# Finch attention with a mixture of adapters on one core: tile 22's scaled r and k transposed by DMA, and the order planned anew

## The chip, the cores and the metric

The kernel runs on one core of a Trainium2 chip. A core has a matrix engine (TensorE: PE for its matmuls, PEld for its weight loads), VectorE (DVE), ScalarE (ACT), GpSimd (POOL), and SyncE (SP), which here only issues DMAs. The metric is the device time of one execution in microseconds; 85.32 us is the median of three before the change.

## The reference

```python
def _attn_ref(r, k, v, w, u):                  # (4, 8, 768, 48) each, u (8, 48)
    state = np.zeros((B, H, D, D))
    for t in range(S):
        cur = einsum('bhd,bhe->bhde', u[None] * kt, vt)
        y[:, :, t] = einsum('bhd,bhde->bhe', rt, state + cur)
        state = wt[:, :, :, None] * state + einsum('bhd,bhe->bhde', kt, vt)

def _moe_ref(x, w_gate, A, B):                 # x = y as (3072, 384); E = 8, rank 16
    logits = x @ w_gate
    # the two largest of 8, softmax over the two
    delta[token] += w_e * ((x @ A[e]) @ B[e])  # for both chosen e
    return x + delta
```

## The kernel before

The 4 x 768 tokens are 24 tiles of 128; six tiles make one sequence (NCHUNK), so the state is started anew at tiles 0, 6, 12 and 18. All work of one tile is cut into small steps. A step is a function, and `PLAN`, a string in the file, lists every step as `name:tile` or `name:tile.variant`; the variant is mostly the engine. The program is emitted in exactly that order, so each engine works through its own steps in the order of the list, and waits where a step's inputs or its buffer are not ready. There is no other scheduling: the list is the schedule.

Steps of one tile t, with their lines:

- `load_w` (L182, L192, from SP), `load_rk` (L203) and `load_v` (L211, both issued by POOL, with a cast to fp16) bring in groups of 2 to 8 tiles; `ln` (ACT, L233, L238) takes the logarithm of w.
- `csA` and `csB` (PE, L245 to L254) sum log w along the tile in a PSUM bank, `expP` and `expN` (ACT, L259, L263) take the exponentials of it and of its negative.
- `mult` (VectorE, L284; L269 in two halves for tiles 0 and 1, there also as `multr`, `multk`) scales r and k by them into one of four buffers `rk2`.
- The scaled r and k must be transposed. `tr` (PE, L332) does it with eight transposes into the PSUM tile `trp`, and `trev` copies that to `rkT` on ACT (L309) or VectorE (variant 1, L311). For some tiles `trd` (L338) does both at once: one DMA transpose on SP's queue, from `rk2` to `rkT`.
- `amm` (PE, L353) multiplies k and r to `a_ps`, which has one buffer; `aev` (VectorE, L359) masks it to `at`; `kv` (PE, L366) adds to the state, `sev` copies the state out (ACT L303, VectorE L305), `szero` (POOL, L382) clears the blocks of the other head.
- `rkp` (L293) is the product r k, on POOL or VectorE (variant 1). `xk` (PE, L421) transposes it together with the result of three tiles earlier, `xkev` copies both out (ACT L309, VectorE L311), `dg` (PE, L298) and `dgev` (L303, L305) give the u term, and `dv` (POOL, L322) multiplies it with v.
- `ymS` (L387) and `ymA` (L397) make y on PE; `ba` (L403) adds dv there with a matmul in variant 1. `xs` is the finished attention row: on ACT (L411) after such a `ba`, else on VectorE, which adds dv to y (L413).
- Mixture: `lg` (PE, L436) makes the logits. For each of eight batches of 4, 4, 4, 4, 4, 2, 1 and 1 tiles follow `g1` (VectorE, from L446), `gexp` (ACT, L461), `g2` to `g4`, `z` (PE, L497), `zw` (VectorE, L505, L510), `zTm` (PE, L520), `zTev` (L309, L311). Then each tile has `d` (PE, L533, L534), `oev` (ACT L303, VectorE L542 or L305) into one of six `res` buffers, and `store` (SP, L546).
- `warm` (PE, L173) are matmuls on constants that keep PE running at the start.

`y_ps`, `xk_ps`, `z_ps`, `zT_ps` and `d_ps` share three PSUM buffers in turn, so such a step waits until the third tile before it in the list has been read out.

```python
    def trd(t, ch):
        x = wk.tile([128, 2, P, 128], BF16, name="rkT", bufs=4)
        nc.sync.dma_start(out=x.rearrange("p m q f -> p (m q) f"),
                          in_=st[t]["rk2"].rearrange("s m p h d -> s (m p h d)"), transpose=True)
```

Of the kernel before, what the change touches and what calls it, by code (L numbers as in the profile page):

```python
# [33 lines left out]
csB:3 expN:3 aev:1 tr:2 ymA:0 kv:2 xk:-1 dv:0.1 ba:0.1 load_rk:12 ln:4 ymS:1 szero:1 ymA:1 trev:2.1 xkev:-1 csA:4
dg:2 xs:0.1 amm:2 rkp:3.1 expP:4 mult:3 xk:0 aev:2 load_w:6 load_v:12 csB:4 sev:2 xkev:0 rkp:4.1 expN:4 tr:3 dg:3
kv:3 csA:5 dv:1.1 trev:3 dgev:3.1 ymS:2 amm:3 expP:5 ymA:2 dv:2.1 ba:1.1 csB:5 mult:4 ln:6 rkp:5 tr:4 sev:3.1 expN:5
aev:3 load_rk:16 xs:1.1 csA:6 trev:4 xk:1 szero:2 expP:6 load_w:8 ba:2.1 amm:4 xs:2.1 mult:5 dv:3 lg:0 szero:3.1
csB:6 tr:5 aev:4 load_w:10 xk:2 expN:6 csA:7 trev:5.1 ymS:3 load_v:16 xkev:1 xkev:2 ymS:4 dg:5 expP:7 ln:8 ymA:3
mult:6 ba:3 dg:4 csB:7 expN:7 load_w:12 rkp:6 amm:5 tr:6 xs:3 xk:3 dgev:5.1 kv:4 lg:2 dv:4 load_w:14 csA:8 trev:6
aev:5 ymA:4 ba:4 sev:4.1 amm:6 expP:8 lg:1 rkp:7 xs:4 szero:4 xkev:3 dv:5.1 csB:8 kv:6 mult:7 lg:3 g1:3 xk:4 expN:8  # L40
ymS:5 csA:9 dg:6 rkp:8 ln:12 xkev:4.1 tr:7 aev:6 load_w:16 expP:9 gexp:3 dg:7 load_B:0 ymA:5 trev:7 z:3 g2:3 ba:5.1
csB:9 dgev:7.1 sev:6 mult:8 expN:9 load_w:18 xs:5.1 amm:7 kv:7 g3:3 lg:4 csA:10 tr:8 ymA:6 sev:7 expP:10 trev:8 kv:8
xk:5 dv:6 aev:7 rkp:9 ba:6 csB:10 g4:3.1 mult:9 tr:9 sev:8 szero:7 kv:9 zw:3 zTm:3 dv:7.1 expN:10 xs:6 zTev:3 csA:11
szero:6 xkev:5 xk:6 trev:9 expP:11 amm:8 ymS:7 xkev:6 mult:10 szero:8 ba:7.1 csB:11 ymA:7 expN:11 dg:9 dg:8 rkp:10
tr:10 aev:8 sev:9.1 xs:7.1 castB:0 csA:12 expP:12 amm:9 ymS:8 dgev:9.1 mult:11 trev:10 xk:7 dv:8 aev:9 rkp:11 csB:12
ymA:8 expN:12 load_w:20 lg:6 tr:11 szero:9 ba:8 d:3.2 xkev:7 trev:11 xs:8 csA:13 lg:7 expP:13 lg:5 oev:3.2 g1:7 d:1
xk:8 csB:13 oev:1 xkev:8.1 expN:13 dv:9 amm:10 d:2 mult:12 ymS:9 csA:14 ba:9 kv:10 dg:10 gexp:7 ymS:10 g2:7 ln:16
ymA:9 aev:10 rkp:13.1 dg:11 dgev:11 tr:12 expP:14 sev:10 oev:2 rkp:12 xs:9 amm:11 dv:10.1 ymA:10 csB:14 aev:11
trev:12.1 expN:14 lg:8 kv:12 mult:13 ba:10.1 rkp:14.1 xs:10.1 g3:7 xk:9 csA:15 d:0.2 szero:10 xk:10 xkev:9 dg:12
expP:15 xkev:10 mult:14 dv:11.1 amm:12 oev:0.2 g4:7 sev:12 szero:12 csB:15 tr:13 expN:15 ymS:11 kv:13 dg:13 ba:11.1  # L50
trev:13 ymA:11 sev:13 csA:16 z:7 xs:11.1 expP:16 tr:14 dgev:13 mult:15 aev:12 zw:7 xk:11 load_w:22 store:0 csB:16
amm:13 lg:10 zTm:7 ymA:12 dv:12 xkev:11.1 ln:20 ba:12 kv:14 lg:11 expN:16 lg:9 trev:14 csA:17 aev:13 dv:13.1 rkp:15
g1:11 ymS:13 zTev:7.1 xs:12 ba:13.1 mult:16 expP:17 sev:14 tr:15 ymA:13 amm:14 xs:13.1 csB:17 gexp:11 xk:12 rkp:16
d:5 szero:13 g2:11 expN:17 xkev:12 xk:13 rkp:18 trev:15 csA:18 trd:16 dg:15 aev:14 expP:18 g3:11 g4:11 dg:14 mult:17
oev:5 z:11 amm:15 csB:18 store:3 dgev:15 kv:15 xkev:13 szero:14 ymS:14 dv:14 rkp:17.1 d:6 expN:18 ymA:14 dv:15 zw:11
csA:19 ba:14 aev:15 sev:15 oev:6 lg:12 ymS:15 szero:15 dg:16 kv:16 lg:13 ymA:15 expP:19 csB:19 ba:15 xs:14 expN:19
amm:16 rkp:19 xk:14 mult:18 zTm:11 sev:16 xs:15 csA:20 kv:18 d:4 xkev:14 aev:16 rkp:21 trd:17 zTev:11.1 xk:15 dg:17
store:1 amm:17 expP:20 ymS:16 oev:4 mult:19 dgev:17 sev:18 ymA:16 csB:20 kv:19 d:8.2 store:2 rkp:22.1 dv:16.1
xkev:15 trd:18 dv:17.1 lg:14 d:11 aev:17 expN:20 ba:16.1 sev:19 csA:21 oev:8.2 mult:20 trd:19 amm:18 xs:16.1 expP:21
lg:15 xk:16 d:9.2 dg:18 csB:21 oev:11 aev:18 szero:16 oev:9.2 ymS:17 rkp:20 ba:17.1 store:5 ymA:17 xkev:16 trd:20  # L60
expN:21 dg:19 kv:20 xs:17.1 amm:19 store:6 csA:22 xk:17 sev:20 szero:19 szero:18 dgev:19 dv:18 mult:21 expP:22 lg:16
kv:21 d:10 xkev:17 ymA:18 csB:22 ba:18 ymS:19 dv:19 aev:19 oev:10 ymA:19 d:7 ba:19 amm:20 g1:15 xs:18 expN:22 xs:19
xk:18 trd:21 gexp:15 xk:19 sev:21 csA:23 oev:7 dg:20 xkev:18 xkev:19 store:9 expP:23 szero:20 rkp:23 ymS:20 lg:17
# [534 lines left out]
```

## Time and profile before

| | before |
|---|---|
| median of 3 runs (lowest, highest) | 85.32 us (85.1, 86.31) |
| the profiled execution | 85.61 us |
| its span, first to last instruction | 83.9 us |
| instructions | 3133 |
| moved by DMA | 19.10 MB |
| granted TensorE clock, mean | 0.988 |

The profile gives for each group of instructions its count, busy time, mean duration and the idle time of the engine just ahead of it. Its times are microseconds from the first instruction. An operation on VectorE begins before the one ahead of it has ended in the record, so durations add up to more than the span; where the order is judged, the distance from one start to the next is the measure. The busy time of PE is modelled from its pipeline and says little on how full it is.

### The profile page before, as it was taken

The page shows a single profiled execution, that of the slowest core. Times are in us where ns is not written, and L with a number is a line of the kernel's source. Part 1 is how long each engine was busy: PE and PEld are TensorE (multiplying, and loading weights), DVE is VectorE, ACT ScalarE, POOL GpSimd, SP SyncE. Part 2 cuts the span into 40 slices and gives each one's busy share as a digit, 9 for nine tenths or more (in the row PEclk, how much of TensorE's full clock was granted, in tenths as well). Part 3 has the DMA queues.
Part 4 walks back from the last instruction along what each step waited for, and adds up shares of the span by engine and source line. Part 5 has one row for each costly group of instructions (what it writes and reads, how often), then busy time and mean ns, then how long its engine had stood idle before and what let it go on. Part 6 is the DMA issues. An engine that isn't in the chain of part 4 may idle for free.

```text
span 83.9 us, 3133 instructions
## 1 busy us (share of the span) xinstructions
PE 76.5 (91%) x1214; PEld 56.8 (68%) x1214; DVE 72.1 (86%) x166; ACT 68.3 (81%) x163; POOL 57.1 (68%) x113
## 2 busy tenths in 40 slices
...
GB/s 13 328 388 283 272 289 281 275 272 293 282 211 214 262 254 252 287 293 283 226 212 212 208 225 55 221 295 140 125 200 225 204 289 90 99 281 109 277 250 129
DMA packets 15407, 19.10 MB, mean 228 GB/s; under 512 B 7200, under 2 KB 12320, under 8 KB 15392
## 3 DMA queue, kind: packets, MB, share of 16 engines
...
q8 instruction: 9, 0.15, 0.7%
...
## 4 chain that ended last, share of the span: by engine, by line
PE 76%; DVE 6%; ACT 6%; DMA 4%; issue 2%; DVEq 1%; ACTq 0%
PE xk_ps L421 10%; PE trp L332 8%; PE a_ps L353 8%; PE y_ps L397 5%; PE cs_ps L254 5%; PE z_ps L497 4%; PE d_ps L534 4%; PE cs_ps L250 4%; PE a_ps L173 4%; DMA w<-in_w_dram 4%; PE s_ps L366 4%; PE y_ps L387 4%; PE cs_ps L245 4%; PE d_ps L533 3%; PE y_ps L403 2%
## 5 line engine op out<-in xcount | busy, mean ns | idle before, releaser
L359 DVE TENSOR_TENSOR at<-a_ps,strict 128x1024 f16<-128x1024 f32 x24 | 29.3, 1220 | 1.2 <-PE a_ps L353 0.8
L322 POOL TENSOR_TENSOR dv<-v,dg 128x384 f16<-128x384 f16 (+1 forms) x24 | 20.4, 859 | 8.6 <-ACT dg L303 4.7
L293 POOL TENSOR_TENSOR rkp<-rk 128x384 f16<-128x384 f16 (+1 forms) x16 | 14.6, 916 | 0.8 <-DMA rk<-in_rk_dram 0.7
L263 ACT ACTIVATE e<-cs_ps 128x384 bf16<-128x384 f32 x24 | 11.9, 494 | 3.3 <-PE cs_ps L254 3.0
L259 ACT ACTIVATE e<-cs_ps 128x384 bf16<-128x384 f32 x24 | 12.1, 503 | 1.6 <-PE cs_ps L250 1.4
L284 DVE TENSOR_TENSOR rk<-rk,e 128x768 bf16<-128x768 f16 x22 | 12.8, 582 | 0.0
L332 PE MATMUL trp<-ident,rk 128*128 128x128 bf16 x144 | 11.1, 219 | 0.4 <-DVE rk L284 0.4
L309 ACT COPY xkT<-xk_ps 128x384 f32<-128x384 f32 (+1 forms) x24 | 10.5, 447 | 0.9 <-PE xk_ps L421 0.6
L382 POOL MEMSET S_sb<- 64x192 bf16 x38 | 9.6, 252 | 2.4 <-DVE S_sb L305 0.5
L332 PEld LDWEIGHTS <-rk 128*128 128x128 bf16 x144 | 9.0, 97 | 2.0 <-DVE rk L284 0.8
L353 PE MATMUL a_ps<-rkT 48*128 48x128 bf16 x192 | 9.5, 219 | 0.1
L309 ACT COPY rkT<-trp 128x512 f32<-128x512 f32 x15 | 9.0, 597 | 0.0
L397 PE MATMUL y_ps<-v,at 128*128 128x48 f16 x192 | 8.7, 183 | 0.0
L250 PE MATMUL cs_ps<-logw,strict 128*128 128x384 f16 x24 | 8.0, 332 | 0.6 <-ACT logw L233 0.6
L303 ACT COPY res<-d_ps 128x384 f32<-128x384 f32 x15 | 7.2, 488 | 1.5 <-PE zT_ps L520 0.9
L353 PEld LDWEIGHTS <-rkT 48*128 48x128 bf16 x192 | 5.5, 94 | 4.1 <-issue 1.8
L293 DVE TENSOR_TENSOR rkp<-rk 128x384 f16<-128x384 f16 (+1 forms) x8 | 3.8, 472 | 5.1 <-DMA rk<-in_rk_dram 5.1
L254 PE MATMUL cs_ps<-logw,ident 128*128 128x384 f16 x24 | 8.0, 335 | 0.2 <-ACT e L259 0.2
L421 PE MATMUL xk_ps<-ident,rkp 128*128 128x128 f16 x72 | 8.0, 220 | 0.0
L421 PE MATMUL xk_ps<-ident,xs 128*128 128x128 f16 x72 | 8.0, 219 | 0.0
L397 PEld LDWEIGHTS <-at 128*128 128x128 f16 x192 | 7.3, 96 | 0.9
L534 PE MATMUL d_ps<-Ball,zT 128*128 128x384 f16 x24 | 7.8, 327 | 0.0
...
## 6 DMA issues: line engine op xcount, KB each, us to landing
...
w_in<-in_w_dram SPq DMA_DIRECT2D x8, 384.0 KB, 13.0
rk<-in_rk_dram POOLq DMA_DIRECT2D x5, 384.0 KB, 14.5
...
w<-in_w_dram SPq DMA_DIRECT2D x3, 384.0 KB, 9.1
v<-in_v_dram POOLq DMA_DIRECT2D x3, 384.0 KB, 18.7
rk<-in_rk_dram POOLq DMA_DIRECT2D x1, 768.0 KB, 21.2
...
```

The lines of the kernel that those rows point to most:

```text
L254: nc.tensor.matmul(cs_ps[:, 0:HD], lhsT=ident16, rhs=st[t]["logw"], start=False, stop=True, skip_group_check=True)
L259: nc.scalar.activation(out=e2[:, 0], in_=cs_ps[:, 0:HD], func=ACT.Exp)
L263: nc.scalar.activation(out=st[t]["e2"][:, 1], in_=cs_ps[:, 0:HD], func=ACT.Exp, scale=-1.0)
L284: nc.vector.tensor_mul(rk2s[t % 4].rearrange("s m p h d -> s (m p h) d")[:, :, 0:D], st[t]["rk"].rearrange("s m (h d) -> s (m h) d", d=D), ...
L293: (nc.gpsimd, nc.vector)[ch].tensor_mul(x, st[t]["r"], st[t]["k"])
L309: nc.scalar.copy(out=out.bitcast(F32), in_=in_.bitcast(F32))
L322: (nc.gpsimd, nc.gpsimd, nc.vector)[ch].tensor_mul(x, st[t]["v16"], st[t]["dg"].rearrange("p (h o) -> p h o", o=1).to_broadcast([L, H, D]))
L332: nc.tensor.transpose(trp[:, m, p, :], st[t]["rk2"][:, m, p, :, :].rearrange("s a b -> s (a b)"), ident)
L353: nc.tensor.matmul(a_ps[:, g, p, :], lhsT=rkT[base:base + D, 1, p, :], rhs=rkT[base:base + D, 0, p, :], start=True, stop=True)
L359: nc.vector.tensor_mul(at, st[t]["a_ps"].rearrange("s g p f -> s (g p) f"), strict.to_broadcast([128, H, 128]))
L397: nc.tensor.matmul(y_ps[:, h, :], lhsT=st[t]["at"][:, g * P + p, :], rhs=st[t]["v16"][:, h, :], start=(c == 0 and h == 0), stop=(h == H - ...
L421: nc.tensor.transpose(xk_ps[:, 3 * q + j, :], src[:, j * 128:(j + 1) * 128], ident16)
```

## The change

Only `PLAN` is edited; no function changes. `tr:22` and `trev:22` go and `trd:22` comes, so that tiles 16 to 22 are transposed by DMA, and 0 to 15 and 23 by PE. All other steps are the same, but their order is new from the first word to the last, and many have another variant. On VectorE are now 14 `rkp` (8 before), 6 `xkev` (3), 3 `sev` (5), 1 `trev` (3), 11 `xs` (12), 8 `oev` (9) and 6 `dgev` (4); POOL has 10 `rkp` (16). The order of POOL's loads among themselves is kept; SP has `load_B` ahead of `load_w:12`. The start and the end of the list:

```diff
-load_w:0 setD:0 warm:0.5 load_w:1.1 load_rk0:1.1 mask_co:0 mask_ident16:0 mask_strict:0 load_v:0 load_rk0:0 table:0
-load_rk:2 ln:0 ln:1 csA:0 warm:1.2 rkp:0.1 load_v:2 expP:0 csB:0 warm:2.3 setid:0 load_rk:4 padD:0 expN:0 multr:0
-load_rk:6 csA:1 warm:3.3 expP:1 csB:1 warm:4.3 multk:0 tr:0 load_w:2 load_wt:0 kv:0 expN:1 ln:2 trev:0 rkp:1
-load_v:4 mult:1 sev:0.1 load_rk:8 csA:2 xk:-3 warm:5.1 load_w:4 amm:0 expP:2 xk:-2 casts:0 load_v:8 csB:2 aev:0 tr:1
...
-aev:20 g2:15 dg:21 lg:18 lg:19 store:7 mult:22 dgev:21 store:11 dv:20.1 amm:21 csB:23 kv:22 z:15 store:10 store:4
-ymA:20 ba:20.1 tr:22 g3:15 ymS:21 expN:23 g4:15 aev:21 xs:20.1 ymA:21 zw:15 dv:21 mult:23 ba:21 xk:20 trev:22 zTm:15
-xkev:20 amm:22 zTev:15.1 g1:19 tr:23 gexp:19 g2:19 xs:21 sev:22 xk:21 aev:22 d:15 dg:23 store:8 dg:22 d:13.2
-szero:21 g3:19 xkev:21 oev:15 z:19 d:14 trev:23 szero:22 g4:19 oev:13.2 amm:23 zw:19 dgev:23 oev:14 dv:22.1 store:15
-d:12 aev:23 store:13 store:14 ymS:22 dv:23 ymA:22 ba:22.1 lg:20 oev:12 lg:21 xs:22.1 g1:21 zTm:19 ymS:23 ba:23
-ymA:23 xs:23 zTev:19.1 xk:22 d:18.2 clr:23 xkev:22 gexp:21 oev:18.2 lg:22 xk:23 store:12 d:19 xkev:23 d:16 oev:19
-g1:22 g2:21 g3:21 lg:23 oev:16 z:21 gexp:22 g1:23 d:17 gexp:23 g4:21 zw:21 zTm:21 g2:22 oev:17 z:22 zTev:21.1 z:23
-g2:23 zw:22 d:21.2 zw:23 d:20 store:18 oev:20 zTm:23 oev:21.2 zTm:22 zTev:22 store:19 zTev:23.1 store:16 d:23.2
-store:17 store:21 oev:23.2 d:22.1 store:20 store:23 oev:22.1 store:22
+setD:0 warm:0.5 padD:0 load_w:0 load_w:1.1 load_rk0:1.1 mask_strict:0 table:0 mask_ident16:0 ln:0 load_v:0 load_rk:2
+load_v:2 load_rk0:0 csA:0 warm:1.2 ln:1 expP:0 load_rk:4 csB:0 warm:2.3 expN:0 mask_co:0 csA:1 warm:3.6 multr:0
+load_rk:6 load_w:2 load_v:4 multk:0 setid:0 expP:1 ln:2 rkp:0.1 tr:0 csB:1 kv:0 warm:4.2 rkp:1.1 trev:0.1 expN:1
+csA:2 amm:0 xk:-2 sev:0 load_rk:8 mult:1 expP:2 xk:-3 aev:0 csB:2 tr:1 xkev:-2.1 load_wt:0 kv:1 load_w:4 expN:2
+csA:3 load_w:6 casts:0 sev:1.1 load_w:8 rkp:3.1 xkev:-3 mult:2 dg:1 expP:3 szero:0 load_v:8 load_rk:10 csB:3 trev:1
+dg:0 amm:1 rkp:2.1 tr:2 dgev:1.1 expN:3 xk:-1 ymA:0 ln:4 trev:2 kv:2 load_rk:12 dv:0.1 csA:4 aev:1 ba:0.1 xkev:-1
+amm:2 ymS:1 expP:4 csB:4 mult:3 load_w:10 xs:0.1 szero:1 sev:2.1 tr:3 expN:4 trev:3 xk:0 xkev:0 dg:2 aev:2 mult:4
+csA:5 ymS:2 kv:3 ymA:1 expP:5 load_v:12 rkp:5.1 ln:6 dg:3 dv:1 szero:2 amm:3 load_B:0 dgev:3.1 ba:1 dv:2.1 csB:5
+tr:4 sev:3.1 ymA:2 xs:1 ba:2.1 expN:5 csA:6 rkp:4.1 lg:0 xk:1 mult:5 trev:4 aev:3 xs:2.1 xk:2 xkev:2.1 expP:6 csB:6
+tr:5 xkev:1 expN:6 dg:4 csA:7 ymS:3 szero:3 mult:6 load_rk:16 load_w:12 dg:5 amm:4 rkp:7.1 dgev:5.1 dv:3 dv:4
+rkp:6.1 trev:5 expP:7 ba:3 lg:1 tr:6 ymS:4 ymA:3 aev:4 csB:7 kv:4 ymA:4 xs:3 ln:8 ba:4 expN:7 amm:5 dv:5 xs:4 csA:8
...
+csB:19 sev:16 d:6 d:11 kv:18 dv:16.1 rkp:18.1 xs:15 expN:19 aev:16 csA:20 oev:6 xk:15 ymS:16 mult:19 dv:17.1 oev:11
+expP:20 amm:17 szero:16 csB:20 ymA:16 ba:16.1 sev:18 trd:18 xkev:15 kv:19 lg:15 ymS:17 rkp:19 store:0 expN:20
...
+szero:19 xk:17 sev:20 trd:21 ymS:19 csA:23 xkev:17 xk:18 dv:19.1 xkev:18 g3:15 g4:15 mult:22 amm:20 ba:19.1 store:11
+ymA:19 aev:20 z:15 kv:21 xs:19.1 dg:21 dg:20 amm:21 xk:19 trd:22 dgev:21 sev:21 zw:15 aev:21 expP:23 szero:20 ymS:20
+rkp:23 kv:22 ymA:20 dv:20 lg:18 zTm:15 store:7 ba:20 dv:21 xs:20 store:6 store:9 szero:21 xkev:19 lg:19 zTev:15.1
+lg:17 csB:23 ymS:21 expN:23 ymA:21 ba:21 xk:20 xkev:20 g1:19 amm:22 xs:21 d:12 dg:22 dg:23 xk:21 store:8 gexp:19
+g2:19 oev:12 mult:23 xkev:21 d:15.2 aev:22 dgev:23 tr:23 sev:22 z:19 trev:23 ymS:22 g3:19 oev:15.2 dv:22.1 ymA:22
+ba:22.1 g4:19 amm:23 d:14 xs:22.1 dv:23 oev:14 zw:19 zTm:19 zTev:19.1 d:13 lg:21 oev:13 lg:20 clr:23 xk:22 d:18
+store:10 szero:22 ymS:23 aev:23 xkev:22 store:12 ymA:23 ba:23 g1:21 xs:23 gexp:21 d:16 g2:21 oev:18 oev:16 lg:22
+z:21 xk:23 store:15 xkev:23 d:17 g3:21 store:14 g4:21 g1:22 zw:21 gexp:22 g2:22 oev:17 zTm:21 d:19 lg:23 zTev:21
+g1:23 oev:19 z:22 store:13 d:21 d:20 zw:22 gexp:23 z:23 oev:21 zTm:22 oev:20 g2:23 zw:23 store:18 zTev:22.1 zTm:23
+d:22.2 zTev:23.1 store:16 store:17 oev:22.2 d:23 store:19 oev:23 store:21 store:20 store:22 store:23
```

More of the change, by code (lines that the diff above doesn't have):

```diff
@@ L28 @@
 PLAN = """
-load_w:0 setD:0 warm:0.5 load_w:1.1 load_rk0:1.1 mask_co:0 mask_ident16:0 mask_strict:0 load_v:0 load_rk0:0 table:0
-load_rk:2 ln:0 ln:1 csA:0 warm:1.2 rkp:0.1 load_v:2 expP:0 csB:0 warm:2.3 setid:0 load_rk:4 padD:0 expN:0 multr:0
-load_rk:6 csA:1 warm:3.3 expP:1 csB:1 warm:4.3 multk:0 tr:0 load_w:2 load_wt:0 kv:0 expN:1 ln:2 trev:0 rkp:1
-load_v:4 mult:1 sev:0.1 load_rk:8 csA:2 xk:-3 warm:5.1 load_w:4 amm:0 expP:2 xk:-2 casts:0 load_v:8 csB:2 aev:0 tr:1
-load_rk:10 expN:2 trev:1 xkev:-2 kv:1 szero:0 xkev:-3 sev:1.1 csA:3 amm:1 mult:2 rkp:2.1 dg:1 dg:0 expP:3 dgev:1
@@ L34 @@
[L34 to L63, printed above, removed]
@@ new lines @@
+sev:4 load_v:16 aev:5 lg:2 szero:4 mult:7 xk:4 trev:6 expP:8 xk:3 csB:8 kv:6 rkp:8 amm:6 xkev:4 expN:8 ymS:5 sev:6
+xkev:3 csA:9 tr:7 load_w:14 expP:9 dg:6 kv:7 lg:3 dg:7 load_w:16 aev:6 trev:7 dgev:7 csB:9 ymA:5 szero:6 ba:5 ymA:6
+expN:9 amm:7 mult:8 rkp:9.1 castB:0 ymS:7 dv:6.1 csA:10 tr:8 g1:3 xs:5 sev:7 gexp:3 expP:10 aev:7 ba:6.1 xs:6.1 xk:5
+dv:7.1 g2:3 csB:10 kv:8 mult:9 trev:8 expN:10 ba:7.1 g3:3 sev:8 xkev:5 xk:6 ymA:7 xs:7.1 amm:8 csA:11 kv:9 tr:9
+szero:7 xkev:6.1 lg:5 expP:11 aev:8 dg:9 rkp:10.1 g4:3 dg:8 z:3 dgev:9.1 dv:8.1 mult:10 csB:11 ymS:8 xk:7 ymA:8 zw:3
```

16 lines of the change are left out of this document (added).

## The prediction

> **What bounds the kernel now.** I read the page's busy shares first, then the busy time in four stretches that I cut at events of VectorE, then the timeline around the cuts. The columns of the second fence are busy microseconds (instructions) of PE, PEld, DVE, ACT and POOL, the granted clock, the DMA share and GB/s.
>
> ```profile
> PE 76.5 (91%) x1214; PEld 56.8 (68%) x1214; DVE 72.1 (86%) x166; ACT 68.3 (81%) x163; POOL 57.1 (68%) x113
> ```
> ```profile
> 0.00:6.89 6.89, 4.89 (x13) 1.76 (x14) 0.76 (x2) 3.20 (x5) 4.94 (x17) 1.00 0.71 248
> 6.89:24.48 17.59, 16.76 (x249) 12.09 (x248) 16.58 (x29) 15.44 (x34) 13.14 (x21) 1.00 1.09 275
> 24.48:73.18 48.70, 48.55 (x880) 39.08 (x878) 47.94 (x110) 45.12 (x111) 37.52 (x73) 1.00 0.90 211
> 73.18:83.91 10.73, 6.28 (x79) 3.83 (x77) 6.84 (x27) 4.55 (x15) 1.51 (x4) 0.91 0.57 211
> ```
>
> 6.89 is VectorE's first work on data, 24.48 its mask of tile 5 (aev:5) and 73.18 the mask of the last tile (aev:23). In the long third stretch VectorE is busy 47.94 of 48.70 us. PE looks as busy, but its matmuls overlap in the record. So the order is costed by VectorE's queue: its work between two events plus its waits. What one operation costs there is the time to the next start, since durations overlap:
>
> ```profile
> 12.25 0.55 DVE L305 CAST S_sb<-s_ps 128x384 bf16<-128x384 f32 x1
> 12.72 0.55 DVE L284 TENSOR_TENSOR rk<-rk,e 128x768 bf16<-128x768 f16 x1
> 13.18 0.35 DVE L293 TENSOR_TENSOR rkp<-rk 128x384 f16<-128x384 f16 x1
> 13.45 1.22 DVE L359 TENSOR_TENSOR at<-a_ps,strict 128x1024 f16<-128x1024 f32 x1
> ...
> L413 DVE TENSOR_TENSOR xs<-dv,y_ps 128x384 f16<-128x384 f32 x12 | 6.5, 545 | 0.1
> L542 DVE TENSOR_TENSOR res<-xs,d_ps 128x384 f32<-128x384 f16 x8 | 4.4, 548 | 0.0
> L311 DVE COPY xkT<-xk_ps 128x768 f16<-128x768 f16 x3 | 1.7, 553 | 0.0
> L489 DVE TENSOR_TENSOR g<-gs,den 128x32 f32<-128x32 f32 x1 | 0.2, 224 | 0.0
> ```
>
> sev costs 0.47 (12.25 to 12.72), mult 0.46, rkp 0.27. xs, oev and xkev last as long as sev (0.55), so 0.47 each.
>
> ```profile
> 20.99 1.23 DVE L359 TENSOR_TENSOR at<-a_ps,strict 128x1024 f16<-128x1024 f32 x1 [0.34 <-PE a_ps L353]
> 22.13 0.68 DVE L311 COPY rkT<-trp 128x1024 bf16<-128x1024 bf16 x1
> 22.73 1.28 DVE L284 TENSOR_TENSOR rk<-rk,e 128x768 bf16<-128x768 f16 x1
> 23.93 0.54 DVE L413 TENSOR_TENSOR xs<-dv,y_ps 128x384 f16<-128x384 f32 x1
> 24.40 0.16 DVE L305 COPY dg<-s_ps 128x16 f32<-128x16 f32 x1
> 24.48 1.21 DVE L359 TENSOR_TENSOR at<-a_ps,strict 128x1024 f16<-128x1024 f32 x1
> ...
> 22.66 0.92 POOL L293 TENSOR_TENSOR rkp<-rk 128x384 f16<-128x384 f16 x1
> 24.64 0.83 POOL L322 TENSOR_TENSOR dv<-v,dg 128x384 f32<-128x384 f16 x1 [1.05 <-DVE dg L305]
> ```
>
> aev costs 1.14, trev 0.60, dgev 0.08. One mult takes 1.28 us instead of 0.55: POOL's rkp began 0.07 us ahead of it. I call that a hold; it costs 0.73.
>
> **Part 1: tile 22 by DMA.** Removed are eight transposes on PE and one copy on ACT, and one DMA transpose is added on SP's queue.
>
> ```profile
> 46.70 0.45 PE trp L332 x8
> L309 ACT COPY rkT<-trp 128x512 f32<-128x512 f32 x15 | 9.0, 597 | 0.0
> ...
> L338 SPq DMA_TRANSPOSE rkT<-rk x6: 1237/1248/1856, 51.0 to 62.7; - x6
> DMA to landing us min/median/max: 3.0/3.1/3.3
> ```
>
> PE loses 0.45 us (and gains 0.16 by one more ba matmul of the new order), ACT loses 0.60. Neither ends the waits of VectorE, so I take nothing for them; the other end is the whole 0.45. The transfer is hidden: in the new VectorE order aev:20, zw:15, aev:21, xs:20, g1:19, xs:21 and mult:23 stand between mult:22 and aev:22. The two masks, two xs and mult:23 alone are 3.7 us, against 3.3 for the landing; zw:15 and g1:19 (some 1.2 more) cover amm:22. Without that cover the overshoot of the landing would count, at most 3.3 us. On SP only store:11 stands directly ahead, whose copy oev:11 is ten ACT operations or more earlier than expN:22; the stores of tiles 7, 6 and 9 stand behind the transpose and its 1.25 us of issue. Of the next writers of their res buffers (oev:18, oev:12, oev:14) only oev:12 comes close to the landing of a store; it may wait an estimated 0.5 us on ACT, which has room.
>
> The Trainium skill ("VectorE: DVE Perf Modes", The three transpose paths) speaks against this edit: it gives 1309 ns for one 128x128 block by DMA and advises TensorE where PSUM will do. Eight blocks one after another would be an estimated 10.5 us and amm:22 would wait some 6; the 3.1 us row decides otherwise.
>
> **Part 2: the new order, up to aev:5.** Now VectorE begins at 6.89 with rkp:0, beside POOL's rkp:1:
>
> ```profile
> 6.89 1.28 DVE L293 TENSOR_TENSOR rkp<-rk 128x384 f16<-128x384 f32 x1 [5.14 <-DMA rk<-in_rk_dram]
> 8.10 0.37 DVE L160 CAST ident<-ident 128x128 bf16<-128x128 f16 x1
> 8.20 1.95 DVE L269 TENSOR_TENSOR rk<-rk,e 128x384 bf16<-128x384 f32 x4
> ...
> 6.76 1.00 POOL L293 TENSOR_TENSOR rkp<-rk 128x384 f16<-128x384 f32 x1 [0.75 <-DMA rk<-in_rk_dram]
> 7.71 0.77 POOL L211 DMA_DIRECT2D v<-in_v_dram  x1
> ...
> v<-in_v_dram POOLq DMA_DIRECT2D x1, 384.0 KB, 16.2
> ```
>
> The first product is held as well (1.28 against 0.55 for the similar L269). In the new order multr:0, multk:0, setid, rkp:0 and rkp:1 come first, POOL issues loads meanwhile, and this hold goes. Counting the new queue ahead of xs:4: five masks 5.7, mult 0 to 6 4.2, eight rkp 2.6, three sev 1.4, two xs 0.9, trev 0.6, two xkev 0.75, setid and three dgev 0.35: 16.5 us, so 23.4; and I allow 0.5 for trev:0, whose transposes stand on PE behind six warm matmuls: 23.9.
>
> But xs:4 needs v of tile 4. That load, issued at 7.71, lands at 23.9 (16.2 later). The order of the loads on POOL's queue is unchanged and the DMA share is 1.09 here, so I let it land then again. dv:4 (0.83) then ends at 24.75, xs:4 starts at 24.85, and aev:5 at 25.3, which is 0.8 later than now. Both ends: 24.4 if the load comes with its earlier issue (the term that DVE's own queue sets), 26.0 with one hold more.
>
> **From aev:5 to aev:23** it now takes 48.70 us. I counted VectorE's operations in this part of both orders. After the change there are three xs (1.41), two sev (0.94), one trev (0.60) and one g4 (0.15) fewer, and two rkp (0.54), two oev (0.94), one xkev (0.47) and one dgev (0.08) more: 1.07 less. With the waits left as they are aev:23 starts at 25.3 + 47.63 = 72.9, against 73.18: -0.25 us. ACT gets two sev, a trev and three xs for it and has 3.6 us free in that stretch.
>
> **After aev:23.** Now the tail is 10.73 us:
>
> ```profile
> 74.94 0.55 DVE L413 TENSOR_TENSOR xs<-dv,y_ps 128x384 f16<-128x384 f32 x1
> 76.63 0.17 DVE L446 MAX8 top<-s_ps 128x8 f32<-128x8 f32 x1
> 80.51 0.55 DVE L305 COPY res<-d_ps 128x384 f32<-128x384 f32 x1
> ...
> 79.55 0.22 PE L520 MATMUL zT_ps<-ident,zw 128*128 128x128 f16 x1 [0.55 <-ACT res L303]
> ```
>
> From the start of the mask, xs:23 is at +1.76, the gate of tile 23 (g1) at +3.45, the last copy ends at +7.88. In the new order the gate is later: two oev copies stand before xkev:23 on ACT, and lg:23 stands behind zTm:21 on PE; I get +4.4. Against that VectorE has three oev fewer behind it (0.47 each), zw:21 is not behind g1:23, and the last zT no longer trails a late oev: gexp:23 near +5.0, zw:23 +5.8, zTev:23 +6.4, last copy ending +7.3. So -0.55; the ends are -0.55 and +0.95, the whole lateness of the gate.
>
> **Sum:** 0 (part 1) -0.25 -0.55 = -0.8. The profiled execution took 85.61 us (span 83.9 and 1.7 around it): 84.8. That execution lies 0.29 above the median of 85.32, so on the scale of the median it is **84.5 us**.
>
> **Rivals.** (a) VectorE runs through: v of tile 4 is not waited for (-0.9) and half of the 0.76 us idle of the third stretch goes: some -1.3 more, 83.2. For it: the load is issued some 2 us earlier. Against: the DMA is full, and the queue ahead of it is the same.
>
> (b) Slower: holds. Rkp on VectorE goes from 8 to 14 operations, each with two SBUF inputs as mult has, and POOL still has 24 dv and 10 rkp. The two maxima below are the only holds so far among 34 such operations of VectorE (22 mult, the 4 of L269, 8 rkp; the mean of mult, 582 ns, is that of 21 at 549 and one at 1282):
>
> ```profile
> L284 DVE TENSOR_TENSOR rk<-rk,e 128x768 bf16<-128x768 f16 x22 | 12.8, 582 | 0.0
> L284 DVE TENSOR_TENSOR rk<-rk,e x22: 525/549/1282, 12.7 to 69.1; 128x768 bf16<-128x768 f16 x22
> L293 DVE TENSOR_TENSOR rkp<-rk x8: 347/352/1283, 6.9 to 57.8; 128x384 f16<-128x384 f16 x7, 128x384 f16<-128x384 f32 x1
> L322 POOL TENSOR_TENSOR dv<-v,dg 128x384 f16<-128x384 f16 (+1 forms) x24 | 20.4, 859 | 8.6 <-ACT dg L303 4.7 <-DVE dg L305 2.6 <-issue 1.1
> ```
>
> Each further one costs 0.73 where VectorE is full, that is between 25 and 73 us. From two on the gain is gone, with four it is +2.9: 87.4; I give three, 86.7. For it: mult and rkp now alternate with masks during which POOL starts its dv. Against: six rkp of 0.91 us leave POOL, and from 24.48 on the profile has no full hold. The Trainium skill ("SBUF — State Buffer", Who interferes with whom) has this rule: a DVE instruction with two SBUF inputs contends with a GpSimd instruction that reads SBUF, and whichever comes first keeps the port for its whole length. The 1.28 us rows agree.
>
> (c) The tail pays: the late gate of tile 23 passes whole to the end, +0.95 instead of -0.55: 86.0. For it: nothing else remains to fill that time. Against: 79.55's wait shows that the present end has slack of its own.
>
> (d) The change does nothing: the waits only change places and the total work of VectorE (the same to 0.2 us by the same count) sets the time: 85.3.
>
> **Chances.** Forecast 0.38, (a) 0.20, (b) 0.17, (c) 0.13, (d) 0.12. The forecast's own range is 83.8 to 85.2. The range over the cases goes from (a) with its idle time gone (82.8) to three holds (86.8). A measurement of this kernel tells about 2%, 1.7 us: under 83.6 lies (a), and a little of the forecast, 0.22; over 87.0 lies four holds, or (b) with (c), 0.16; the rest, 0.62, is within.
>
> **What would show it.** Right: multr first on VectorE at 6.9, aev:5 near 25.3 behind xs:4 and a wait that ends with the load of v; aev:23 near 73; tile 22's transpose issued near 65 and landed before amm:22 in about 3.1 us; g1 of tile 23 more than 4 us after aev:23. It is wrong if VectorE idles more than 1 us between 25 and 73 us, if mult or rkp rows of 1.2 us appear there, or if amm:22 waits for SP's transfer.

## The result, and the profile after

The change makes the kernel slower. Its median is 88.48 us (88.34 to 88.89 in four runs); the kernel before, run beside it, has 85.24 us (85.10 to 86.31). The ratio is 1.036, 95% interval 1.027 to 1.045. Some executions of a kernel fall into a slower state; all ratios leave them out, and the one profile of e1_best below is of such an execution, so that only the landings of its transposes are read from it. The forecast was 84.5 us, with a range of 82.8 to 86.8: the sign was wrong, and the time lies beyond the range, on the side to which the prediction gave a chance of 0.16.

Two lines of the page of after and one of its groups answer to those shown of before: the busy times of the engines, and `mult` on VectorE (busy us, mean ns of one).

```profile
span 86.8 us, 3112 instructions
PE 76.9 (89%) x1208; PEld 56.4 (65%) x1208; DVE 72.4 (83%) x168; ACT 69.5 (80%) x163; POOL 52.4 (60%) x110
...
L284 DVE TENSOR_TENSOR rk<-rk,e 128x768 bf16<-128x768 f16 x22 | 13.7, 625 | 0.0
```

The span is 2.9 us longer, and no engine got 2.9 us more work. The busy time in stretches (columns as before), now cut at 25.32, the mask of tile 5 (aev:5), and at 75.32, that of tile 23 (aev:23), says where the time went:

```profile
25.32:75.32 50.00, 47.92 (x860) 38.11 (x857) 48.56 (x110) 44.50 (x108) 35.08 (x70) 1.00 0.90 207
75.32:86.83 11.51, 6.36 (x70) 3.61 (x68) 5.71 (x24) 5.62 (x17) 1.08 (x5) 0.93 0.52 191
```

Up to aev:5 the kernel lost 0.84 us (25.32 for 24.48), from there to aev:23 1.30 (50.00 for 48.70), behind aev:23 0.78 (11.51 for 10.73): 2.92 together. The first was forecast. Against the forecast the second stretch is 2.37 too long (50.00 for 47.63) and the third 1.33 (11.51 for 10.18). Four things in the trace stand out. First, the chain that ended last (start, us, what) passes through two `mult` operations of 1.3 us and through one transpose by DMA of 4.84:

```profile
5.48 18.37 DMA v<-in_v_dram
...
50.99 1.36 DVE rk L284
...
54.28 1.31 DVE rk L284
...
58.06 4.84 DMA rkT<-rk
```

Second, the timeline beside those two `mult` shows in each case a product of GpSimd that starts just then:

```profile
50.90 1.44 DVE L284 TENSOR_TENSOR rk<-rk,e 128x768 bf16<-128x768 f16 x1
52.27 0.17 DVE L482 TENSOR_REDUCE den<-gs 128x4 f32<-128x32 f32 x1
54.28 1.31 DVE L284 TENSOR_TENSOR rk<-rk,e 128x768 bf16<-128x768 f16 x1
55.51 0.54 DVE L413 TENSOR_TENSOR xs<-dv,y_ps 128x384 f16<-128x384 f32 x1
...
51.02 0.90 POOL L293 TENSOR_TENSOR rkp<-rk 128x384 f16<-128x384 f16 x1
54.35 0.82 POOL L322 TENSOR_TENSOR dv<-v,dg 128x384 f32<-128x384 f16 x1
```

From start to next start these take 1.37 and 1.23 us where 0.46 is usual: 0.91 and 0.77 lost. They are tiles 16 and 17, beside rkp:17 and dv:15. Third, the late transpose is tile 18's; its amm waits for it, and aev:18 for that:

```profile
DMA to landing us min/median/max: 3.1/3.2/4.8
```

(that was the row of all seven transposes of after; the timeline shows who waits)

```profile
62.94 0.40 PE L353 MATMUL a_ps<-rkT 48*128 48x128 bf16 x8 [0.55 <-DMA rkT<-rk]
63.38 1.23 DVE L359 TENSOR_TENSOR at<-a_ps,strict 128x1024 f16<-128x1024 f32 x1 [0.70 <-PE a_ps L353]
```

Fourth, the end. The timeline has xs:23, the gate g1:23, the last copy (oev:23) and the last store:

```profile
77.45 0.55 DVE L413 TENSOR_TENSOR xs<-dv,y_ps 128x384 f16<-128x384 f32 x1 [0.47 <-PE y_ps L397]
...
79.86 0.18 DVE L446 MAX8 top<-s_ps 128x8 f32<-128x8 f32 x1
...
82.53 0.48 ACT L303 COPY res<-d_ps 128x384 f32<-128x384 f32 x1 [0.47 <-PE d_ps L534]
83.44 0.33 SPq L546 DMA_DIRECT2D out_dram<-res  x1
```

and the DMA issues of a window around 83.44 its landing (KB, us):

```profile
out_dram<-res SPq DMA_DIRECT2D x1, 192.0 KB, 2.5
```

The copy ends at 83.01, the store is issued 0.43 us later and lands 2.46 later. In the kernel before the last copy ended at 81.06, and the last store's rows in the same two views were:

```profile
81.09 0.34 SPq L546 DMA_DIRECT2D out_dram<-res  x1
```
```profile
out_dram<-res SPq DMA_DIRECT2D x1, 192.0 KB, 1.9
```

### The profile page after: what moved, and what is told of

It is laid out like the page before. It is cut to its first block, busy times and chain, and to the rows that moved or that the text cites. A ratio compares the mean times of both kernels' runs of the same rounds, so it can differ in the third digit from the quotient of the medians.

```text
span 86.8 us, 3112 instructions
## 1 busy us (share of the span) xinstructions
PE 76.9 (89%) x1208; PEld 56.4 (65%) x1208; DVE 72.4 (83%) x168; ACT 69.5 (80%) x163; POOL 52.4 (60%) x110
## 4 chain that ended last, share of the span: by engine, by line
DMA 27%; DVE 25%; PE 21%; ACT 10%; POOL 7%; issue 4%; POOLq 0%; DVEq 0%; ACTq 0%
DMA v<-in_v_dram 21%; DVE at L359 9%; DMA rkT<-rk 6%; DVE rk L284 5%; PE a_ps L353 3%; PE d_ps L534 2%; DVE res L542 2%; PE xk_ps L421 2%; POOL dv L322 2%; DVE xs L413 2%; PE y_ps L397 2%; POOL rk L203 2%; PE d_ps L533 2%; DVE zw L510 2%; ACT logw L238 2%
## 5 line engine op out<-in xcount | busy, mean ns | idle before, releaser
L322 POOL TENSOR_TENSOR dv<-v,dg 128x384 f16<-128x384 f16 (+1 forms) x24 | 19.9, 839 | 13.2 <-ACT dg L303 5.2
L382 POOL MEMSET S_sb<- 64x192 bf16 x40 | 10.1, 252 | 6.9 <-ACT S_sb L303 3.8
L284 DVE TENSOR_TENSOR rk<-rk,e 128x768 bf16<-128x768 f16 x22 | 13.7, 625 | 0.0
L309 ACT COPY xkT<-xk_ps 128x384 f32<-128x384 f32 (+1 forms) x21 | 9.4, 452 | 1.4 <-PE xk_ps L421 1.3
L332 PE MATMUL trp<-ident,rk 128*128 128x128 bf16 x136 | 10.4, 219 | 0.0
L309 ACT COPY rkT<-trp 128x512 f32<-128x512 f32 x16 | 9.5, 595 | 0.0
L293 POOL TENSOR_TENSOR rkp<-rk 128x384 f16<-128x384 f16 x10 | 9.2, 923 | 0.0
L303 ACT CAST S_sb<-s_ps 128x384 bf16<-128x384 f32 x17 | 8.4, 492 | 0.5 <-POOL dv L322 0.4
L173 PE MATMUL a_ps<-ones 128*128 128x512 f16 x18 | 6.6, 500 | 1.4 <-DVE ones L143 1.4
## 6 DMA issues: line engine op xcount, KB each, us to landing
rk<-in_rk_dram POOLq DMA_DIRECT2D x1, 768.0 KB, 23.9
```

The source lines that it names most:

```text
L284: nc.vector.tensor_mul(rk2s[t % 4].rearrange("s m p h d -> s (m p h) d")[:, :, 0:D], st[t]["rk"].rearrange("s m (h d) -> s (m h) d", d=D), ...
L303: nc.scalar.copy(out=out, in_=in_)
L309: nc.scalar.copy(out=out.bitcast(F32), in_=in_.bitcast(F32))
L322: (nc.gpsimd, nc.gpsimd, nc.vector)[ch].tensor_mul(x, st[t]["v16"], st[t]["dg"].rearrange("p (h o) -> p h o", o=1).to_broadcast([L, H, D]))
L332: nc.tensor.transpose(trp[:, m, p, :], st[t]["rk2"][:, m, p, :, :].rearrange("s a b -> s (a b)"), ident)
L382: (nc.gpsimd, nc.vector)[ch].memset(st[t]["S"][64 - 64 * g:128 - 64 * g, g], 0.0)
```

## The experiments

Four theories were set against one another. H: holds, that is, VectorE's two-input operations stopped by GpSimd's products. D and F: the late DMA transpose. T and S: the tail, by a wait of ymS:23 or by the place of the last store in SP's queue. One table holds what the traces of all kernels gave: the start of aev:5, the distances from it to aev:18 and aev:23, the rest of the span behind aev:23 (the tail), the span, and the ratio to the kernel before on the same chip. The ratios come from all runs of a kernel, the other columns from the one profiled execution.

| kernel | aev:5 at | to aev:18 | to aev:23 | tail | span | ratio (95%) |
|---|---|---|---|---|---|---|
| before | 24.48 | 35.95 | 48.70 | 10.73 | 83.9 | 1 |
| after | 25.32 | 38.06 | 49.99 | 11.51 | 86.8 | 1.036 (1.027 to 1.045) |
| a1_hold | 25.26 | 36.34 | 48.27 | 11.43 | 85.0 | 1.011 (1.007 to 1.015) |
| a2_tr22 | 25.36 | 37.46 | 49.72 | 10.59 | 85.7 | 1.024 (1.017 to 1.031) |
| b1_trd22 | 24.62 | 35.95 | 48.71 | 10.70 | 84.0 | 0.997 (0.992 to 1.002) |
| a3_tail | 25.13 | 38.00 | 49.93 | 11.10 | 86.2 | 1.026 (1.020 to 1.032) |
| r1_order | 25.18 | 37.43 | 49.36 | 11.37 | 85.9 | 1.026 (1.021 to 1.031) |
| a4_split | 25.80 | 37.98 | 49.91 | 10.84 | 86.5 | 1.032 (1.027 to 1.036) |
| b2_split | 24.32 | 35.95 | 48.76 | 11.68 | 84.8 | 1.012 (1.006 to 1.018) |
| c1_all | 25.18 | 37.48 | 49.41 | 10.60 | 85.2 | 1.017 (1.008 to 1.026) |
| c2_all | 25.05 | 36.65 | 48.58 | 11.13 | 84.8 | 1.011 (1.007 to 1.016) |
| c3_all | 25.24 | 36.62 | 48.88 | 10.61 | 84.7 | 1.013 (1.009 to 1.017) |
| d1_before | 23.42 | 36.83 | 49.58 | 10.74 | 83.7 | 0.997 (0.994 to 0.999) |
| f1_fetch | 26.24 | 37.66 | 50.52 | 11.12 | 87.9 | one run of 89.58 us, no interval |
| f2_fetch | 25.49 | 38.10 | 50.03 | 11.44 | 87.0 | 1.041 (1.032 to 1.049) |
| e1_best | - | - | - | - | - | 0.996 (0.991 to 1.001) |

The distances between masks repeat within about a tenth of a microsecond from kernel to kernel where nothing in between was edited; the start of aev:5 moves by some tenths, up to 0.75 between kernels with one order up to there (25.05 in c2, 25.80 in a4). So the distances are compared, not the spans.

**a1_hold: the two products of GpSimd out of the way.** The kernel leaves out rkp:17 and dv:15 and writes zeros instead.

```diff
-        (nc.gpsimd, nc.vector)[ch].tensor_mul(x, st[t]["r"], st[t]["k"])
+        if t in (17,): nc.gpsimd.memset(x, 0.0)
+        else: (nc.gpsimd, nc.vector)[ch].tensor_mul(x, st[t]["r"], st[t]["k"])
# and the same in dv for t == 15
```

> The kernel after, with the products rkp of tile 17 and dv of tile 15 on GpSimd replaced by writes of zeros of the same size (those two products are left out). Theory H (VectorE is held when a GpSimd operation that reads SBUF starts within about 0.1 us of a VectorE operation with two SBUF inputs): both long mult rows (1.44 us at 50.9 and 1.31 us at 54.3) go back to 0.55, aev:23 starts 1.66 us earlier than in the kernel after (near 73.7 instead of 75.3) and the time falls by 1.4 to 1.7 us, to about 87.0. Theory D (the lateness comes from the DMA transposes): the rows become short, but the transposes of tiles 17 to 20 are then waited for instead and the time falls by less than 0.6 us. Theory T (the tail costs it): aev:23 may be earlier, the stretch after it stays at 11.5 us.

The row of `mult` (min/median/max ns), and then the stretch from aev:5 to aev:23:

```profile
L284 DVE TENSOR_TENSOR rk<-rk,e x22: 545/548/559, 12.7 to 70.5; 128x768 bf16<-128x768 f16 x22
```
```profile
25.26:73.53 48.27, 47.53 (x859) 38.20 (x857) 46.89 (x110) 44.34 (x108) 34.19 (x70) 1.00 0.93 214
```

Both long rows are gone and the stretch is 1.72 us shorter. One of the two writes of zeros, that for rkp:17, starts beside a `mult` (0.10 us behind it) and holds nothing:

```profile
50.83 0.55 DVE L284 TENSOR_TENSOR rk<-rk,e 128x768 bf16<-128x768 f16 x1
50.93 0.41 POOL L294 MEMSET rkp<- 128x384 f16 x1
```

The other starts at 54.18, behind its `mult` (53.31), and says nothing on this. The transpose of tile 18 still took 4.77 us, and the tail stayed at 11.43: H has its 1.7 us, and no more.

**a2_tr22 and b1_trd22: the tile of the title alone.** In a2 the order of after has tile 22 on TensorE; in b1 the order of before has it on DMA.

```diff
# a2 (from after)
-... xk:19 trd:22 dgev:21 ...      +... xk:19 dgev:21 ...
-... kv:22 ymA:20 ...              +... kv:22 tr:22 ymA:20 ...
-... xkev:19 lg:19 ...             +... xkev:19 trev:22 lg:19 ...
# b1 (from before): trd:22 behind mult:22, tr:22 and trev:22 out
```

> The kernel after, with tile 22 alone transposed on TensorE again (eight transposes behind kv:22, the copy trev:22 on ScalarE behind xkev:19; no trd:22); everything else as after. Theory H: tile 22's transpose is not on the path, the time stays within 0.4 us of the kernel after (88.5). Theory D, if tile 22 is the cause: the time falls by 1.5 us or more. Theory T: the same within 0.4 us, tail 11.5 us.

> The kernel before, with tile 22 alone transposed by DMA (trd:22 behind mult:22, no transposes on TensorE and no copy trev:22); the order of everything else as before. Theory H: the half of the change that its first words name is hidden, the time is that of the kernel before within 0.4 us (85.3), and tile 22 lands before its amm has room. Theory D, if tile 22 is the cause: slower by 1 us or more.

In b1 nothing happened: 48.71 us between the masks, a tail of 10.70, no ratio to be told from 1, and all seven transposes in time:

```profile
DMA to landing us min/median/max: 3.1/3.1/3.2
```

In a2 the time fell, by 1.2 us of span in the profiled execution (85.7; its three other runs had 86.2 to 86.4), which no theory had expected in this size. It did not come from tile 22: from aev:18 to aev:23 a2 is even 0.33 us longer (12.26 for 11.93), so the DMA transpose of tile 22 by itself helps in this order. Two other things changed. Tile 18's transpose landed in time, which made aev:18 0.60 us earlier, and the tail lost 0.92 us, because the last store again followed its copy (end at 82.81) at once. First the landings of its six transposes, then the timeline:

```profile
DMA to landing us min/median/max: 3.1/3.1/3.5
```
```profile
58.10 1.24 SPq L338 DMA_TRANSPOSE rkT<-rk  x1
...
82.33 0.48 ACT L303 COPY res<-d_ps 128x384 f32<-128x384 f32 x1 [0.47 <-PE d_ps L534]
82.83 0.36 SPq L546 DMA_DIRECT2D out_dram<-res  x1
```

**a3_tail: the wait of ymS:23.**

```diff
-... clr:23 xk:22 d:18             +... clr:23 xk:22
-... store:12 ymA:23 ba:23 ...     +... store:12 ymA:23 d:18 ba:23 ...
```

> The kernel after, with d:18 moved behind ymA:23 in the order, so that ymS:23 takes a PSUM ring buffer that is not waiting for oev:13 on ScalarE. Theory T: xs:23 then starts 1.8 us after aev:23 instead of 2.13, the idle 0.47 us of VectorE ahead of it goes, and the time falls by 0.3 to 0.5 us. Theory H: at most 0.4 us of the 3.2 us lost lies there. If the tail's length is set by something else behind xs:23 (the gate, the last copies, the last store), the time stays as after, within 0.15 us.

As T says: xs:23 now at 76.81, 1.75 us behind aev:23 (75.06) and with no wait ahead of it; the tail is 0.41 us shorter.

```profile
76.81 0.55 DVE L413 TENSOR_TENSOR xs<-dv,y_ps 128x384 f16<-128x384 f32 x1
```

**r1_order: the holds avoided with all the work kept.**

```diff
-dv:13 szero:14 ... g2:11 ... rkp:16 ... rkp:17 aev:14 ... szero:15 dv:15
+dv:13 rkp:16 szero:14 ... g2:11 rkp:17 ... aev:14 ... dv:15 szero:15
```

> The kernel after, complete, with two pairs of GpSimd's work in another order: rkp:16 ahead of szero:14 and rkp:17 right behind g2:11 (so that neither begins beside mult:16), and dv:15 ahead of szero:15 (so that it doesn't begin beside mult:17). Theory H: no mult row over 0.6 us is left, aev:23 starts 1.6 to 1.8 us earlier than in the kernel after (75.3), like the run without the two products, and the span is near 85.0 instead of 86.8. If it were the products themselves and not the moment at which they start, the rows of 1.4 and 1.3 us would stay or move to another operation, and the span with them.

A miss, and an instructive one. The hold of tile 16 went; but rkp:16, moved ahead, now fell beside mult:15 and held that, and mult:17 was still held in part, by dv:15, which now started 0.31 us ahead of it:

```profile
47.57 0.91 POOL L293 TENSOR_TENSOR rkp<-rk 128x384 f16<-128x384 f16 x1
47.61 1.28 DVE L284 TENSOR_TENSOR rk<-rk,e 128x768 bf16<-128x768 f16 x1
...
53.68 0.83 POOL L322 TENSOR_TENSOR dv<-v,dg 128x384 f32<-128x384 f16 x1
...
53.99 0.94 DVE L284 TENSOR_TENSOR rk<-rk,e 128x768 bf16<-128x768 f16 x1
54.84 0.54 DVE L413 TENSOR_TENSOR xs<-dv,y_ps 128x384 f16<-128x384 f32 x1
```

So 0.73 us of the 1.72 were given back in another place, and 0.39 (0.85 from start to next start, for 0.46) stayed in the old one. That leaves 0.60, and the stretch is 0.63 shorter (49.36). It is not the product that costs, but the moment at which it starts.

**a4_split and b2_split: the place of the last store.** In the record of the kernels before, a2 and b1 SP stands still for some 0.45 us ahead of its 80th instruction, a wait behind the last store. In after the transpose of tile 22 and its wait stand ahead of all that, and the 80th instruction is the last store. a4 puts four instructions more ahead, so that another instruction falls there; b2 does to b1 what the change did to the order of after.

```diff
+        n = {3: 3, 2: 3}.get(t, 1)       # a4; in b2 {0: 3}, from b1
+        for i in range(n):
+            c = slice(i * HD // n, (i + 1) * HD // n)
-        (nc.sync, nc.scalar)[ch].dma_start(out=out[t * 128:(t + 1) * 128, :], in_=st[t]["res"])
+            nc.sync.dma_start(out=out[t * 128:(t + 1) * 128, c], in_=st[t]["res"][:, c])
```

> The kernel after with the first two stores (tiles 3 and 2, issued near 47 us, where SP's queue is otherwise idle) each cut into three of a third of the columns: four instructions more on SP's queue. Theory S (SP's queue has a stop of about 0.45 us ahead of its 80th instruction in the record, of before and of after alike; the added transpose and its wait moved the last store onto it): the last store is now issued within 0.05 us of its copy's end instead of 0.43, and the time falls by 0.4 us, or by up to 1.0 us if its landing is 1.85 us again instead of 2.46. If the late store hangs on the copy on ScalarE or on the DMA of tile 22 itself, nothing changes, or it is slower by a little for four more instructions.

> The kernel before with tile 22 transposed by DMA (as the run b1) and its first store (tile 0, near 46 us) cut into three: two instructions more on SP's queue than in b1, so that the last store becomes the 80th instruction in the record, as in the kernel after. Theory S: the last store is issued 0.45 us after its copy's end instead of 0.03 and the span is 0.4 to 1.0 us longer than b1's 84.0. If the stop isn't tied to the place in SP's queue: 84.0 as b1.

Last copy and last store of a4, then of b2 (copy ends at 83.40 and 80.99):

```profile
82.92 0.48 ACT L303 COPY res<-d_ps 128x384 f32<-128x384 f32 x1 [0.47 <-PE d_ps L534]
83.42 0.36 SPq L549 DMA_DIRECT2D out_dram<-res  x1
```
```profile
80.44 0.55 DVE L305 COPY res<-d_ps 128x384 f32<-128x384 f32 x1
81.42 0.34 SPq L549 DMA_DIRECT2D out_dram<-res  x1
```

In a4, with more instructions, the store follows at once, and the tail falls by 0.67 us; the ratio hardly shows it (1.032), as aev:5 started 0.47 us later there. In b2 the store is issued 0.43 us late and the tail grows by 0.98 over b1's. (In b2 the last store is the 81st instruction in the record; the stop is ahead of its wait, the 80th.) For the late issue S holds in both directions. Not all of b2's 0.98 is the stop: 0.39 is the late issue and 0.22 the landing (2.07 for 1.85), but 0.36 lies between the landing and the end of the span (1.27 for 0.91). The four kernels with split stores have 1.15 to 1.27 us there and the others 0.90 to 0.98, so the split seems to cost something itself.

In after, 0.40 is the late issue (0.43 for 0.03), and the landing takes 0.61 more (2.46 for 1.85). What the traces add: in all sixteen kernels an instruction fetch of 8 KB on queue q14 begins 0.63 to 1.06 us behind the start of SP's 80th instruction (in after at 84.50, during the last store). In the nine kernels in which that instruction is a store, it landed after 2.08 to 2.48 us, and the store ahead of it after 1.81 to 1.92. This speaks for a fixed place in SP's program at which the queue first stops and then fetches, and for the fetch as what delays the landing; the fetch was never moved by itself, so this is not shown.

**c1_all, c2_all, c3_all: the parts together.** c1 is r1, a3 and a4. c2 has the holds avoided by giving rkp:17 to VectorE, with a3 and a4. c3 is a2 with rkp:17 on VectorE and a3.

```diff
# c2, c3 (from after, from a2)
-... g3:11 rkp:17 aev:14 ...       +... rkp:17.1 g3:11 aev:14 ...
```

> The kernel after, complete, with the three things put together: GpSimd's order as in r1, d:18 behind ymA:23, and the first two stores each cut into three. If the three costs are separate they add: 1.8 (holds) + 0.4 (wait of ymS:23) + 0.4 to 1.0 (last store) off the kernel after's span of 86.8, so 83.6 to 84.2; beside 83.9 of the kernel before, within 0.4 us of it. If they cover one another, it stays near r1's 85.0.

> The kernel after, complete: rkp of tile 17 on VectorE behind mult:16 (0.27 us more there, and nothing of GpSimd beside mult:16 and mult:17), d:18 behind ymA:23, the first two stores each cut into three. If the costs add: no mult row over 0.6 us, aev:23 at 73.8 (75.32 less 1.79 plus 0.27), a tail of 10.6 as in c1, span 84.4: beside 83.9 of the kernel before, a ratio of 1.00 to 1.01. If a hold appears elsewhere again, as in r1, 0.7 us more.

> The order of after without tile 22's DMA transpose (TensorE does it, as in a2), complete: rkp of tile 17 on VectorE and d:18 behind ymA:23. If the costs add: 85.7 (a2) less 1.66 plus 0.27 for the holds, less 0.35 for the wait of ymS:23: a span of 84.0, so that the new order alone, freed of its holds, would be level with the kernel before. If a hold appears elsewhere, 84.7.

The costs add in the main, but not enough. In c1 the tail is 10.60 (0.91 less), and the masks keep both holds of r1. c2 has no hold left and 1.41 us less between the masks (1.72 less the 0.27 of rkp:17 would be 1.45); its tail is 11.13, since xs:23 waits again, now 2.12 us behind aev:23. c3 was to get 84.0 and got 84.7, as tile 18's transpose was late there once more (4.77 us), unlike in a2. Freed of its holds and with the last store in place the new order is still 1.1 to 1.3% slower than the kernel before. Most of that is the start, with aev:5 0.6 to 0.8 us later; and tile 18's transpose is late in both c2 and c3.

**d1_before, f1_fetch, f2_fetch, e1_best: the late transpose.** d1 takes the hold at 22.73 us out of the kernel before. f1 and f2 put tiny matmuls in place of the first warm ones, to move the fetches of TensorE's instructions (queue q8, 16 KB each). e1 is d1 with three tiny ones.

```diff
# d1 (from before): ... load_v:16 ... rkp:6 ...  ->  ... rkp:6 load_v:16 ...
# f1 (from after): warm:0.5 -> warm:0.1 and 20 matmuls 128x8; f2: warm:0.4 and 4; e1: 0.4 and 3
```

> The kernel before, complete, with one pair of GpSimd's instructions swapped: rkp:6 ahead of the issue of the load of v of tile 16 (so that it starts near 21.9 us, and not at 22.66 beside mult:6). Theory H: mult:6 takes 0.55 instead of 1.28 us, aev:5 starts up to 0.73 us earlier than 24.48, and the span falls by 0.3 to 0.7 us, to 83.2 to 83.6; the ratio is near 0.994. If a wait for the load of v of tile 4 (landed at 23.9) takes the place of the hold, the span stays at 83.9.

> The kernel after with four of the five first warm matmuls of TensorE replaced by twenty tiny ones (128x8), in about the same time: sixteen matmuls and their weight loads more, so that each later fetch of TensorE's instructions falls about 1 us earlier in its work. Theory F (the transpose of tile 18 lands 1.7 us late, 4.84 instead of 3.1, because a 16 KB fetch of instructions, 0.93 us long, sits on one DMA engine while the transpose's last packets are due there): with the fetch moved, that transpose lands in 3.1 to 4.0 us, or another one is late instead. If its lateness comes from the order of the transposes on SP's queue, it stays at 4.7 to 4.9 us. The time of the whole is left open: the holds and the last store may move with the start.

> The kernel after with one of the five first warm matmuls of TensorE replaced by four tiny ones (128x8): three matmuls and their weight loads more, which moves each later fetch of TensorE's instructions some 0.2 to 0.3 us earlier in its work, and nothing else. Theory F (a fetch that starts 2.63 to 2.87 us after the transpose's issue makes it late): the fetch now starts 2.6 us or less after the issue of tile 18's transpose, that lands in 3.1 to 3.2 us and not in 4.84, the mask of tile 18 starts 37.4 instead of 38.06 us after that of tile 5, and the time falls by 0.3 to 0.6 us. If the order of the transposes makes it late: 4.7 to 4.9 us as before. If the last store moves with the start by chance, the end says less than these two marks.

> The kernel before, complete, with rkp:6 ahead of the issue of the load of v of tile 16 (as d1), and one of the five first warm matmuls replaced by three tiny ones. In d1 the hold at 22.7 us went (0.73 us gained), but the transpose of tile 18 landed 4.64 us after its issue instead of 3.03 (0.64 us lost; its fetch started 2.63 us after the issue). Theory F: with four more instructions of TensorE the fetch starts 2.4 to 2.6 us after it, the transpose lands in 3.1 us, the masks of tiles 5 to 23 take 48.9 instead of 49.58 us, and the span falls from 83.7 to about 83.1: a ratio of 0.988 to 0.992. If the fetch isn't the cause: 83.7 as d1.

In d1 `mult` of tile 6 took 0.55 us and aev:5 started at 23.42; but tile 18's transpose, in time in before, landed after 4.64 us, and 0.64 us of the gain went there (0.24 more went between aev:5 and aev:6, which was not followed up). Of all versions it is the only one whose interval lies below 1, by 0.1 to 0.6%. Its `mult` of tile 6 in the timeline, and the landings of its transposes:

```profile
22.39 0.55 DVE L284 TENSOR_TENSOR rk<-rk,e 128x768 bf16<-128x768 f16 x1
```
```profile
DMA to landing us min/median/max: 3.1/3.2/4.6
```

In f1 the fetch started 1.29 us behind the issue of tile 18's transpose (after: 2.82), and this landed after 4.00 us; in its place tile 21's, with a fetch 2.87 us behind its issue, took 4.90. The DMA queues in three short windows of f1 show tile 21's issue at 65.66 (window 65.6 to 65.7), its fetch (68.5 to 68.6), and tile 18's transpose under way beside its own fetch (60.4 to 60.5, the last two rows):

```profile
rkT<-rk SPq DMA_TRANSPOSE x1, 4.9
...
q8 instruction: 1, 0.02, 57.6%
...
q8 instruction: 1, 0.02, 58.0%
rkT<-rk SPq DMA_TRANSPOSE x1, 4.0
```

f2 failed as an experiment: the fetch did not move (2.85 us behind the issue), and the transpose landed after 4.86 us as before. In e1 the fetch was 2.53 us behind and the transpose landed in 3.19 us; its ratio of 0.996 (0.991 to 1.001) is d1's. Over all kernels tile 18's transpose was late (4.6 to 4.9 us) in each one with a fetch 2.63 to 2.85 us behind its issue, and in time in each one with a fetch 2.51 to 2.59 us behind. In these ten, and for tile 21 in f1, the landing came 2.0 to 2.1 us behind the start of the fetch. That the lateness goes with the fetch is thus well supported, and f1 moved both. Why 0.04 us should decide it stays open, and the border is not the same for every tile: in b1 a fetch began 2.63 us behind the issue of tile 21's transpose, which landed after 3.07.

## Why the prediction was wrong

**The start was right.** `multr` came first on VectorE, aev:5 at 25.32 (25.3 forecast), behind xs:4 and a wait for dv:4 that goes back to the load of v: issued at 5.48, landed at 23.86. The landing of 23.9 "then again" held although the issue was 2.2 us earlier, and rival (a) fell with that. That it agrees to 0.02 us is partly luck: the kernels with the same order up to there started aev:5 between 25.05 (c2) and 25.80 (a4).

**From aev:5 to aev:23: the count was right, the waits were not left as they are.** 47.63 was forecast, 50.00 came. Without the holds it is 48.27 (a1), and a2 shows 0.60 for the late transpose: 48.27 - 0.60 = 47.67, 0.04 from the forecast (worked out from two runs; no one kernel has both out). The step that failed is "with the waits left as they are": it put the new order's waits at those of before, and the runs show 1.72 us of holds and 0.60 us of a late transpose more. Rival (b) named the mechanism, its price (0.73; here 0.77 and 0.91) and the count from which the gain is gone (two; two came). (The upper end of its range, 86.8, is 86.7 by its own sum.) It had a chance of 0.17, because before showed no full hold behind 24.48; but the starts of a new order are new draws, and r1 drew one more by a shift of one product. The Trainium skill ("SBUF — State Buffer", Who interferes with whom) says, of VectorE's modes that use both ports, that whoever issues first gets the shared pair for the whole instruction. The traces agree on the contention of two-input operations with GpSimd's reads (in a1 a write alone held nothing), and not on who wins if that is read from the recorded starts: `mult` started 0.12 and 0.07 us ahead of GpSimd's product and was still held, until 0.42 us after the product's end. An estimate from these rows: as a free `mult` takes 0.55 us in all, a held one seems to have done the first 0.13 us of its record before it needs what the product has, and a product that starts within these 0.13 us still comes first.

**Part 1: "hidden" was right for the transfer and wrong for SP's queue.** Tile 22's transpose landed in 3.4 us and amm:22 did not wait for it; b1 costs nothing. What I left out is that it adds two instructions to SP's queue, which in the new order put the last store on a stop of that queue: 0.43 us late in its issue. Off the stop, the tail is 0.67 us (a4) and 0.92 us (a2) shorter; put onto it, it is 0.98 longer (b2, 0.36 of it behind the landing). In b1's order the same two instructions hit nothing.

**The late transpose of tile 18** was in no step and no rival: I took the landing of 3.0 to 3.3 us as fixed, from six transposes. It costs 0.6 us.

**The tail: +0.78 instead of -0.55.** The gate at +4.54 (4.4 forecast), zw:23 at +5.85 (5.8) and zTev:23 at +6.53 (6.4) were each a little late, and the last copy ended at +7.69 (7.3). That is 0.39 of the 1.33; the wait of ymS:23 for oev:13's ring buffer explains it (a3: 0.41). The other 0.97 is from the copy's end to the span's: 3.82 us for 2.85, the last store. (The two make 1.36, as the prediction put -0.55 for 7.3 - 7.88 = -0.58.) The sum took that end as fixed. Rival (c) was right on the side, not on the place: the late gate is the small part.

Together: 0.02 (start) + 1.72 (holds) + 0.60 (tile 18) + 0.04 + 0.39 (ring) + 0.97 (last store) = 3.74 us, against 3.72 between the forecast's span (83.1) and the measured one (86.8) (the rest is rounding).
